# Where the first two tail loads and the last batch's turns stand in SyncE's queue

## The chip, the cores and the metric

The kernel runs on one core of a Trainium2 chip. The metric is the device time of one execution in microseconds (us). Durations inside an execution come from one profiled execution; its times count from the first instruction of the program. The engines are TensorE (PE; its weight loads are PEld), VectorE (DVE), ScalarE (ACT), GpSimd (POOL) and SyncE (SP). Each takes its instructions in the order in which the program lists them, and all of this kernel's transfers but one small one at the start are issued by SP.

## The reference

Eight batches of eight heads, 576 positions, head size 64. Retention (attention with a decaying causal mask, no softmax), then a feed-forward layer with a Swish whose slope is given for each hidden unit.

```python
scores = scale * np.matmul(q, k.transpose(0, 1, 3, 2))
gamma = 1.0 - 2.0 ** (-5.0 - np.arange(H, dtype=np.float32))
rel = pos[:, None] - pos[None, :]
Dmat = np.where(rel >= 0, gamma[:, None, None] ** rel[None, :, :], 0.0)
ret = scores * Dmat[None, :, :, :]
attn_out = np.matmul(ret, v).astype(np.float32)
x = attn_out.transpose(0, 2, 1, 3).reshape(B * S, H * D)      # 4608 x 512
h = x @ w_in                                                  # 512 -> 2048
g = h * (1.0 / (1.0 + np.exp(-beta * h)))
out = (g @ w_out).astype(np.float32)                          # 2048 -> 512
```

## The kernel before

**Blocks.** The 576 positions of a batch are cut into 512 and a rest of 64. The rests of the eight batches make a ninth block of 8 x 64 = 512 positions, the tail, so that the feed-forward layer works on nine blocks of 512 positions. They are done in the order 0 to 6, then 8 (the tail), then 7 (the last batch).

**Retention of a batch.** Queries and keys are multiplied by powers of the decay beforehand, so that a score needs only a triangular mask. The scores are worked out in chunks of 64 positions; what earlier chunks give comes through a running state (`d_st`). `scores(u)` (line 979) puts on TensorE the states' second half and the scores of batch u, and on VectorE their masks; `outputs(u)` (line 986) puts on it the products with the values, the products of the queries with the states, and the next batch's first states. For the tail (u = 8) a chunk of 128 rows holds the rests of two batches, each with its own final state.

**How inputs get there.** For each batch:

- `load_q` (line 75): two transfers of 512 KB, the queries; `pre_q` (line 282) scales them into bf16 `qs` on GpSimd.
- `load_kv` (line 87): for each of four chunks of 128 positions two transfers of 256 KB, keys and values; `pre` (line 301) casts the keys into `kn` and scales the values into `vn` on GpSimd.
- `x_q` and `x_k` (lines 338 and 343): a *turn*, a transposing DMA within the core (line 336) that makes from two chunks of `qs` the half of `qT`, from two chunks of `kn` the pair's `kT`. The scores need the turned tensors; the states need `kn` and `vn` alone.

For the tail:

- `load_tail(t)` (line 111), t = 0 to 3: six transfers of 128 KB (line 122), two each of queries, keys and values, into buffers of the ring `kvn` that the batches' chunks use too (six buffers).
- `pre` for a tail chunk (lines 310 to 320): seven GpSimd operations that scale the queries and cast the keys into one tile, and scale the values.
- `x_tail` (line 347): one turn for queries and keys together.

**The order.** Nothing is scheduled at run time: `merged` (line 796) walks through a list `fill` of feed-forward pieces and puts in other steps by a number that each carries: a step numbered x is written out ahead of the first piece whose place n is x or more. A step's instructions go to the end of each engine's queue at that point, and SP's queue is kept in exactly this order, waits included:

```python
while todo and todo[0][0] <= n:
    todo.pop(0)[1]()
f()
```

The pieces of block m are 16 `up` (first matrix and Swish, line 732) and 16 `down` (second matrix, line 766: four quarters for each of four results of 128 rows). With the last quarter of a result VectorE copies it out of PSUM (line 783) and SP stores it (line 789). Block 5 takes the places 176 to 207: its `up` pieces 176 to 191, its `down` pieces 192 to 207, and its four stores stand with the pieces 195, 199, 203 and 207. Block 6 begins at 208, the tail at 240, block 7 at 272.

**The numbers around the change.** `pair_prep` (line 1003) gives the steps of a pair of chunks their numbers, relative to `at`, the time at which the pair is due. For the last batch (b = 7) `at` is 211 for its first pair and 218 for its second; the tail's steps are set against `lo6` = 211. `scores(7)` stands at 218, `outputs(7)` at 223.5, the tail's scores at 231.5 and its outputs at 236.5. GpSimd's preparations of the last batch's four chunks stand at 191, 192, 194 and 195, those of the tail's four at 199, 203, 208 and 212.

Of the kernel before, what the change touches and what calls it, by code (L numbers as in the profile page):

```python
# [19 lines left out]
def kernel(  # L20
# [11 lines left out]
    B, H, S, D = q.shape  # L32
# [36 lines left out]
    XB = 2  # L69
# [736 lines left out]
    def F(f, *a):  # L806
        return lambda: f(*a)
# [195 lines left out]
    def pair_prep(i, at):  # L1003
        b, c = seq[i]
        if b is None:
            early, late = ((-23, -12, -7), (-18.5, -8, -6.5)) if c == 0 else ((-11, -3, 7.5), (-6, 1, 8))
            return [(lo6 + x, f) for j, at3 in enumerate((early, late))
                    for x, f in zip(at3, (F(load_tail, c + j), F(pre, i + j), F(x_tail, i + j)))]
        n, st = full.index(i), []
        if b == XB:  # L1010
            if c == 0:
                return [(d0 + 13, F(pre, i + x, (0,))) for x in range(2)] + \
                       [(d0 + 14, F(pre, i + x, (1,))) for x in range(2)]
            return [(u1 + 13.1, F(pre, i + x)) for x in range(2)]
        if c == 0:
            if b == XB + 1:
                st += [(at - 30.1, F(x_k, XB, 1)), (at - 30, F(load_kv, n)), (at - 30, F(load_kv, n + 1))]
            sooner = 4 if b == B - 1 else 0
            st += [(at - 30 - sooner, F(load_q, b, (u,))) for u in range(2)] + [(at - 20 - sooner + x, F(pre_q, b, x)) for x in range(4)]
            st += [(at - (18 if b > B - 3 else 14) + 1.5 * x, F(x_q, b, x)) for x in range(2)]  # L1020
        early = b == XB + 1 and c > 0
        loads = [] if b == XB + 1 and c == 0 else [(at - 29.7 + x / 10, F(load_kv, n + x)) for x in range(2)] if early else \
            [(at - 28 + 2 * x - (7 if b == B - 1 and c else 5 if b == B - 1 else 4 if b == B - 2 and c else 0), F(load_kv, n + x)) for x in range(2)]
        soon, turn_k = (24 if c else 20, 19 if c else 15.5) if b == B - 1 else (22, 11.5) if b == XB + 1 and c == 0 else (16, 13 if c else 11.5)
        return st + loads + [(at - soon, F(pre, i)), (at + 1 - soon, F(pre, i + 1)), (at - turn_k, F(x_k, b, c // 2))]

    for n in range(1, B - 1):
        lo, hi = (base[n] + 17, base[n + 1] - 9.5) if n == 1 else (base[n] + 3, base[n + 1] - 14)
        at = (lo, hi)
        work = [(n + 1, hi - 1, hi + 6.5)]  # L1030
        if n == B - 2:
            at = (lo, lo + 7, lo + 14, lo + 18)
            work = [(B - 1, lo + 7, lo + 12.5), (B, lo + 20.5, lo + 25.5)]
        for x, t in enumerate(at):
            streams.append(pair_prep((n + 1) * CB + 2 * x, t))
        if n == 1:
            work = []
            on_scalar.add((1, 0))
            streams.append([(base[2] - 12, F(scores_with_states, XB, XB)), (hi + 6, F(outputs, XB))])
        for u, t, t2 in work:  # L1040
            streams.append([(t, F(scores, u)), (t2, F(outputs, u))])
# [31 lines left out]
```

## Time and profile before

| | us |
|---|---|
| Three runs | 295.15, 294.44, 294.72 |
| Their median | 294.72 |
| The profiled execution | 294.68 |
| Its span, first to last instruction | 293.0 |
| Block 5, `up` from | 171.99 |
| Block 5, `down` from | 185.80 |
| Block 6, `up` from | 202.53 |
| Scores of the last batch from | 211.53 |
| Scores of the tail from | 225.67 |
| The tail's block, `up` from | 234.66 |
| Block 7, `up` from | 262.28 |

The times of blocks and scores are those of the chain of waits in order of time, the chain that ended last, followed back from the last instruction. The mean granted TensorE clock is 1.000. In the groups of the page and in the timelines a line gives start (in the timelines), duration, engine and line, operation, what is written from what, and how many instructions are put together; `SPq` is SP's queue, where the duration is that of the issue and not of the transfer. "To landing" is from the issue's start to the arrival of the data.

### The profile page before, as it was taken

What the parts mean: (1) busy time and instruction counts of PE and PEld (TensorE: products, weight loads), DVE (VectorE), ACT (ScalarE), POOL (GpSimd) and SP (SyncE); (2) the same over time, 40 slices, a digit from 0 to 9 for tenths busy, and PEclk for the clock granted to TensorE, in tenths of its full rate; (3) what the DMA queues carried; (4) which work ended last, traced back from release to release, by engine and by line L of the source; (5) the groups of instructions that cost most, each with busy time, mean ns of one, the idle gap of its engine ahead of it and who ended that gap; (6) DMA issues with size and microseconds to landing.
All of it is one profiled execution on the core that took longest, in us unless ns stands there. A gap on an engine that the chain in (4) does not pass through costs nothing.

```text
span 293.0 us, 7966 instructions
## 1 busy us (share of the span) xinstructions
PE 287.3 (98%) x3404; PEld 147.3 (50%) x3404; DVE 103.9 (35%) x223; ACT 146.5 (50%) x263; POOL 110.0 (38%) x219
## 2 busy tenths in 40 slices
PE   8899999999999999999999999999999999999995
PEld 3544456875544554455445544554554544444443
DVE  5864566606620650065105520453063500110012
ACT  5665537883487235733473348434780168007600
POOL 3956037852751914371419506773323000000000
PEclk9999999999999999999999999999999999999999
DMA  7999999999999999949999949999998110131011
GB/s 232 306 369 384 378 266 260 218 141 194 272 195 287 253 167 246 239 68 166 242 239 196 190 122 250 197 176 203 209 165 143 74 38 0 36 72 38 0 72 72
DMA packets 121986, 53.99 MB, mean 184 GB/s; under 512 B 97744, under 2 KB 114400, under 8 KB 121952
## 3 DMA queue, kind: packets, MB, share of 16 engines
q1 hardware_dynamic: 121920, 53.49, 81.3%
q8 instruction: 26, 0.43, 0.7%
q14 instruction: 8, 0.07, 0.1%
q10 hardware_dynamic: 32, 0.01, 0.0%
HBM read 36.71 MB, written 9.44 MB: 158 GB/s over the span
## 4 chain that ended last, share of the span: by engine, by line
PE 91%; DMA 5%; SPq 2%; DVE 1%; issue 0%
PE po L776 43%; PE ph L739 38%; DMA wt<-in_moe_w_in_dram 3%; PE ph L754 2%; DMA kvn<-in_v_dram 2%; PE sc L493 2%; SPq L104 2%; PE O L547 2%; PE st L515 1%; PE O L562 1%; PE ph L917 0%; SPq L84 0%; PE T L354 0%; DVE w_in_sb L214 0%; PE sc L627 0%; PE T L611 0%
## 5 line engine op out<-in xcount | busy, mean ns | idle before, releaser
L776 PE MATMUL po<-w_out_sb,gT 128*128 128x512 bf16 (+2 forms) x593 | 128.4, 373 | 0.0
L741 ACT ACTIVATE gT<-ph,beta_sb 128x512 bf16<-128x512 f32 (+1 forms) x144 | 91.3, 643 | 48.9 <-PE ph L739 48.8
L739 PE MATMUL ph<-xT,w_in_sb 128*128 128x512 bf16 (+1 forms) x576 | 113.7, 357 | 0.7 <-DVE sum L881 0.7
L776 PEld LDWEIGHTS <-gT 128*128 128x128 bf16 x593 | 56.2, 98 | 64.1
L739 PEld LDWEIGHTS <-w_in_sb 128*128 128x128 bf16 x576 | 55.9, 98 | 56.0 <-issue 0.7
L783 DVE COPY ot<-po 128x512 f32<-128x512 f32 (+2 forms) x32 | 21.5, 672 | 72.3 <-PE po L776 72.3
L499 DVE TENSOR_TENSOR R<-sc,tri 128x512 bf16<-128x512 f32 x30 | 18.7, 683 | 70.9 <-PE sc L493 70.9
L298 POOL TENSOR_TENSOR qs<-qn,gq 128x256 bf16<-128x256 f32 (+1 forms) x36 | 26.5, 765 | 35.5 <-DMA qn<-in_q_dram 35.5
L328 POOL CAST kn<-kvn 128x128 bf16<-128x128 f32 (+1 forms) x78 | 22.7, 330 | 32.4 <-DMA kvn<-in_k_dram 32.4
L308 POOL TENSOR_TENSOR vn<-kvn,gv 128x512 bf16<-128x512 f32 x26 | 27.1, 1045 | 5.1 <-DMA kvn<-in_v_dram 4.3
L576 ACT CAST xT<-O 128x512 bf16<-128x512 f32 x14 | 7.5, 589 | 32.0 <-PE O L562 32.0
L527 ACT CAST sbd<-warm 128x256 bf16<-128x256 f32 x18 | 7.3, 405 | 21.6 <-DVE warm L523 15.2
L754 PE MATMUL ph<-xT,w_in_sb 128*128 128x512 bf16 x56 | 12.6, 379 | 0.0
L523 DVE TENSOR_TENSOR warm<-st,first 128x256 f32<-128x256 f32 x20 | 8.4, 422 | 9.7 <-PE st L515 8.4
L523 DVE TENSOR_TENSOR first<-st,warm 128x256 f32<-128x256 f32 x25 | 10.6, 425 | 2.5
L576 DVE CAST xT<-O 128x512 bf16<-128x512 f32 x14 | 9.0, 687 | 5.3 <-PE O L562 5.3
L757 ACT ACTIVATE gT<-ph,beta_sb 128x512 bf16<-128x512 f32 x14 | 8.5, 687 | 4.1 <-PE ph L754 4.1
L315 POOL TENSOR_TENSOR kn<-tln,gq 128x128 bf16<-128x128 f32 (+1 forms) x12 | 5.7, 472 | 12.9 <-PE ph L739 7.1
L212 POOL CAST w_in_sb<-wt 128x256 bf16<-128x256 f32 (+1 forms) x15 | 8.0, 547 | 5.0 <-DMA wt<-in_moe_w_in_dram 5.0
L754 PEld LDWEIGHTS <-w_in_sb 128*128 128x128 bf16 x56 | 5.4, 98 | 6.2 <-POOL w_in_sb L212 0.2
L527 ACT CAST sbd<-first 128x256 bf16<-128x256 f32 x18 | 7.3, 405 | 2.2 <-DVE first L523 0.2
L229 DVE TENSOR_SCALAR w_out_sb<-wt,rbeta_sb 128x512 bf16<-128x512 f32 x13 | 5.9, 484 | 5.1 <-DMA wt<-in_moe_w_out_dram 5.1
(136 smaller groups left out, 166.9 us busy)
## 6 DMA issues: line engine op xcount, KB each, us to landing
qn<-in_q_dram SPq DMA_DIRECT2D x16, 512.0 KB, 5.3
kvn<-in_k_dram SPq DMA_DIRECT2D x32, 256.0 KB, 5.7
kvn<-in_v_dram SPq DMA_DIRECT2D x32, 256.0 KB, 5.2
out_dram<-ot SPq DMA_DIRECT2D x31, 256.0 KB, 3.7
wt<-in_moe_w_out_dram SPq DMA_DIRECT2D x8, 512.0 KB, 9.4
wt<-in_moe_w_in_dram SPq DMA_DIRECT2D x5, 512.0 KB, 10.0
wt<-in_moe_w_in_dram SPq DMA_DIRECT2D x6, 256.0 KB, 6.1
tln<-in_q_dram SPq DMA_DIRECT2D x8, 128.0 KB, 3.8
```

The lines of the kernel that those rows point to most:

```text
L298: nc.gpsimd.tensor_tensor(batch[b]["qs"][:, cs, to], q_tiles[b][:, hs, cs].rearrange("p h i d -> p i h d"), gq[:, cs, hs].unsqueeze(3).to_ ...
L308: nc.gpsimd.tensor_tensor(live[i]["vn"], kv_tiles.pop(i)[:, 1], gains(gv, c), ALU.mult)
L328: nc.gpsimd.tensor_copy(kn[:, c % 2, to], t[:, 0, hs])
L499: nc.vector.tensor_tensor(R[x][:, j].rearrange("k c p q -> k (c p) q"), sc[j].rearrange("k c p q -> k (c p) q"), mask, ALU.mult)
L523: nc.vector.tensor_tensor(new[:], add, sums[(c - 1) % 2][:], ALU.add)
L527: e((sbq[c] if c < NC - 1 else ends[u])[:], new[:])
L576: es[n % 2](x, o)
L739: nc.tensor.matmul(ph, w_in_sb[:, ko, fo * P:(fo + 1) * P], xts[m][:, ko, :, w], start=(ko == 0), stop=(ko == KO - 1))
L741: nc.scalar.activation(gts[m][:, fo, :, w], ph, ACT.Silu, scale=beta_sb[:, fo:fo + 1])
L754: nc.tensor.matmul(phs[f][:], w_in_sb[:, ko, f * P:(f + 1) * P], xts[m][:, ko], start=(ko == 0), stop=(ko == KO - 1))
L776: nc.tensor.matmul(po[:, x:y], gT[:, fo, ms, :], w_out_sb[:, fo, n0 + x:n0 + y], start=(fo == 0), stop=(fo == FO - 1), skip_group_check=m < 2)
L783: (nc.scalar.copy if m == 0 or (m, ms) in on_scalar else nc.vector.tensor_copy)(ot, po[:, :nn])
```

## The change

Four numbers in `pair_prep` are changed. No step is added or taken away, and no step itself is changed.

```diff
         if b is None:
-            early, late = ((-23, -12, -7), (-18.5, -8, -6.5)) if c == 0 else ((-11, -3, 7.5), (-6, 1, 8))
+            early, late = ((-15.9, -12, -7), (-15.85, -8, -6.5)) if c == 0 else ((-11, -3, 7.5), (-6, 1, 8))
...
-            st += [(at - (18 if b > B - 3 else 14) + 1.5 * x, F(x_q, b, x)) for x in range(2)]
+            st += [(at - (15.8 if b == B - 1 else 18 if b > B - 3 else 14) + (0.1 if b == B - 1 else 1.5) * x, F(x_q, b, x)) for x in range(2)]
...
-        soon, turn_k = (24 if c else 20, 19 if c else 15.5) if b == B - 1 else (22, 11.5) if b == XB + 1 and c == 0 else (16, 13 if c else 11.5)
+        soon, turn_k = (24 if c else 20, 22.95 if c else 18.9) if b == B - 1 else (22, 11.5) if b == XB + 1 and c == 0 else (16, 13 if c else 11.5)
```

The numbers that result:

| Step | before | after |
|---|---|---|
| First tail chunk, `load_tail(0)` | 188 | 195.1 |
| Second tail chunk, `load_tail(1)` | 192.5 | 195.15 |
| Query turns of the last batch | 193 and 194.5 | 195.2 and 195.3 |
| First key turn of the last batch | 195.5 | 192.1 |
| Second key turn of the last batch | 199 | 195.05 |

SP's queue from the last batch's last key and value load to the third tail chunk:

- before: loads of tail chunk 0, loads of tail chunk 1, two query turns, store of block 5's first result, two key turns, store of the second result, loads of tail chunk 2;
- after: first key turn, store of block 5's first result, second key turn, loads of tail chunk 0, loads of tail chunk 1, two query turns, store of the second result, loads of tail chunk 2.

From tail chunk 2 on the queue is as before: its six loads, a store, the turns of chunks 0 and 1, the loads of chunk 3, a store, the turns of chunks 2 and 3. The order on the other engines, and the buffers that the tiles take, are not touched.

## The prediction

> **What bounds the kernel now.** I read the page's busy times and its chain of waits first, then the timelines of SyncE's queue (SP), GpSimd (POOL), VectorE (DVE) and TensorE (PE) around the moved steps, and last the single turns.
>
> ```profile
> PE 287.3 (98%) x3404; PEld 147.3 (50%) x3404; DVE 103.9 (35%) x223; ACT 146.5 (50%) x263; POOL 110.0 (38%) x219
> PE 91%; DMA 5%; SPq 2%; DVE 1%; issue 0%
> ```
>
> TensorE sets the end. Only 293.0 - 287.3 = 5.7 us of the span are not matmul time, and in the chain, told in order of time, TensorE's groups join without a break from 81.17 to 289.96 us. So there is almost nothing to win behind the start; a moved transfer can only cost, and it costs when TensorE comes to something that has not landed.
>
> The queue that the change rearranges (start, duration, line, what is issued; x2 means two in a row):
>
> ```profile
> 187.50 1.81 SPq L122 DMA_DIRECT2D tln<-in_q_dram  x2
> 189.41 2.23 SPq L122 DMA_DIRECT2D tln<-in_k_dram  x2
> ...
> 193.05 1.31 SPq L122 DMA_DIRECT2D tln<-in_q_dram  x2
> ...
> 197.56 3.22 SPq L336 DMA_TRANSPOSE qT<-qs  x2
> 200.88 0.52 SPq L789 DMA_DIRECT2D out_dram<-ot  x1
> 201.51 2.66 SPq L336 DMA_TRANSPOSE kT<-kn  x2
> 204.25 0.53 SPq L789 DMA_DIRECT2D out_dram<-ot  x1
> 204.84 1.34 SPq L122 DMA_DIRECT2D tln<-in_q_dram  x2
> ...
> 212.50 2.16 SPq L122 DMA_DIRECT2D tln<-in_q_dram  x2
> 214.71 1.31 SPq L122 DMA_DIRECT2D tln<-in_k_dram  x2
> ...
> 218.15 4.26 SPq L336 DMA_TRANSPOSE kT<-kn  x2
> ```
>
> The reader is to see that SP hardly rests: from 187.50 to 218.10 one issue follows the other within 0.7 us. A tail load is 0.63 us for its 128 KB when nothing holds it, a turn 1.28. Each later issue is late by whatever is put ahead of it.
>
> ```profile
> 191.70 0.68 DVE L783 COPY ot<-po 128x512 f32<-128x512 f32 x1
> ...
> 184.81 0.88 POOL L328 CAST kn<-kvn 128x256 bf16<-128x256 f32 x3
> ...
> 190.22 0.88 POOL L328 CAST kn<-kvn 128x256 bf16<-128x256 f32 x3
> ...
> 220.86 0.29 POOL L316 CAST kn<-tln 128x128 bf16<-128x128 f32 x1
> ...
> 211.36 0.87 PE L493 MATMUL sc<-qT,kT 64*64 64x64 bf16 x64
> ...
> 225.60 0.74 PE L493 MATMUL sc<-kT 64*64 64x64 bf16 x64
> ```
>
> The copy at 191.70 makes the first result of block 5; its store (L789) stands in SP's queue between moved steps. The casts end the last batch's key pairs at 185.69 and 191.10. The matmuls at 211.36 are the last batch's scores, which need its turned queries and keys; those at 225.60 are the tail's scores, which need all four tail turns. The last of these is the closest:
>
> ```profile
> L336 SPq DMA_TRANSPOSE kT<-kn x1: 1232/1232/1232, 221.2 to 221.2; - x1
> DMA to landing us min/median/max: 4.1/4.1/4.1
> ```
>
> Issued at 221.18 (it waited for the cast that ends at 221.15), it lands at 225.3. The tail's scores go through four chunks of 16 matmuls in 0.67 us (225.67 to 226.34 in the chain), and only the last chunk reads this turn, so TensorE needs it at about 226.0. **The slack is 0.7 us**, the smallest of all moved steps.
>
> **The change, part by part.** No instruction is added or removed: 12 tail loads, two key turns and two query turns change places on SP. GpSimd's, VectorE's, ScalarE's and TensorE's order stay as they are, and so do the buffers each load takes.
>
> *The two key turns, ahead of the loads.* The first is issued at about 187.5, where the loads began: its keys are cast since 185.69. It takes 1.28 us unhindered, and 3.47 as the turn at 180.47 did behind four loads; I need not choose, since either ends by 191.0. The second is placed just behind the store of block 5's first result (fill 195), and that store waits for the copy that ends at 191.70 + 0.68 = 192.38. **This is the new wait**: before, the store came to the head at 200.88, long ready. Now SP stands idle for between 192.4 - 191.0 = 1.4 and 192.4 - 188.8 = 3.6 us, and the second key turn, 12 loads and two query turns stand behind it. The keys themselves are far too early to matter (needed at 211.4).
>
> *SP from 192.38 on.* By start to start in the rows: the store 0.63 (200.88 to 201.51); the key turn 1.38 (201.51 to 202.89); two tail chunks of six loads, 4.11 each (193.05 to the end of the waits at 197.16); two query turns, 3.72 (197.16 to 200.88) if they are hindered behind 12 loads as now, 2.76 if they go like two key turns; the second store 0.59 (204.25 to 204.84). Sum: 0.63 + 1.38 + 8.22 + 3.72 + 0.59 = 14.54, or 13.58. The third tail chunk then starts at 206.92 or 205.96, where it starts at 204.84 now: **later by 2.1 or 1.1 us**. Whether the queue's load then is nearer to the one row or the other can't be read, because it has drained during the new wait and is then filled by the same 12 loads; I take the middle, 1.6.
>
> *The tail's first two chunks.* They are issued 7 to 9 us later. Their keys land with 3.5 to 4.7 us after issue at 201 and 205; GpSimd's 1.6 us of casts (194.87 to 196.45) end by 207, and their own turns are issued about 211 and 213 either way: covered by 4 us.
>
> *The query turns.* The second is issued at 202.4 + 1.6 = about 204 to 205 instead of 199.47. Turns here land 3.1 to 6.3 us after issue, so at 207 to 211.3, against 211.36 when TensorE asks. Nothing is paid, but at the far end the cover is gone; each tenth beyond it would be a tenth of TensorE's.
>
> *What is late next.* From the third chunk on SP keeps its order: six loads, a store, two turns, six loads, a store, two turns. The last chunk's second key load (issued at 215.39) is what GpSimd's last casts (219.57 to 221.15) wait for, and they release the last turn. So 1.6 us goes through whole: the last turn lands at 225.3 + 1.6 = 226.9, and TensorE waits 1.6 - 0.7 = **0.9 us** for it. Bounds: one issue in this stretch holds SP longer than its kind (1.48 against 0.63 at 212.50); if it goes freely, the shift shrinks by 0.85, and 1.1 - 0.85 - 0.7 is below nothing, so no cost; if another load behind the query turns is held like that, 2.1 + 0.85 - 0.7 = 2.25 us. A gain is excluded to within half a microsecond: the batch's chain shows short matmul groups stretched at 195.5 (0.40 and 0.43 against 0.29 and 0.25 a batch earlier) and at 211.5 (0.70 against 0.58), 0.4 us together, all there is to recover.
>
> *TensorE behind it.* Nothing absorbs the wait: the masks, outputs and the last two blocks follow in its order, so a late 0.9 us arrives whole at the end.
>
> The sum: the profiled execution took 294.68 us (span 293.0 and 1.7 around it), against a median of 294.72; 294.68 + 0.9 = 295.6 us.
>
> **A rule weighed against the rows.** A turn's issue took 1.28 us where a load's took 0.63. The Trainium skill (Advanced Engine Details and Errata, section "X-Bar Transpose (TRN2)") says that transposing DMAs are as fast as regular ones on this chip; by that the three turns of the sum would be issued like loads, which is the rival "turns as loads" below. The traces so far speak against it as far as the issue goes.
>
> **Rivals.**
>
> *The slack holds* (not slower). One mechanism: after the drain at 189 to 192.4 SP issues the rest unhindered (query turns 1.38 each, no 1.48 load), the last turn is 0.3 to 0.7 us later than now and still lands before 226.0. For it: 206 to 208 us shows that the transfers do thin out now and then, and the rows at 187.50 and 190.05 hold backlog (1.14 and 1.59 us issues) that the wait would clear. Against it: the two turns behind 12 loads are the very sequence that was hindered. It decides below a shift of 0.7 us; the time is that of before, 294.7.
>
> *Turns as loads* (not slower). If three turns cost 0.68 each from start to start, the sum is 0.63 + 8.22 + 0.59 + 2.04 = 11.48, the third chunk starts at 203.9, 1.0 us earlier than now, and nothing is paid: 294.7. All eight turns between 197 and 222 took 1.23 us or more; little chance.
>
> *The query turns become the wait* (slower still). If they land 6.3 us after an issue at 205.5 or later, TensorE stands at the last batch's scores too; with the shift of 2.1 us and more behind it this gives 1.5 to 2.5 us: 296.2 to 297.2. For it: the one turn that took 6.3 us came behind six loads and a store. Against it: those behind 12 loads took 3.9.
>
> *The batch's small bubbles go* (faster): the 0.4 us named above, 294.3 us; only together with something that no row shows would it be past 0.2%.
>
> **How the numbers follow.** The forecast, a wait of 0.4 to 1.5 us at the tail's scores: 0.55; the slack holds: 0.26; turns as loads: 0.02; queries late: 0.12; bubbles: 0.05. A difference of 0.2%, 0.59 us, is about what a measurement of this kernel can tell. Of the forecast's case some 0.08 lies below that; so slower 0.47 + 0.12 = 0.59, same 0.26 + 0.02 + 0.08 = 0.36 (the bubbles alone give 0.01 more and the rest of theirs faster): 0.59, 0.37 and 0.04. The range must reach down to the case without a cost and up into the late queries: 294.5 to 296.6.
>
> **What would show it.** In the changed profile: a store of L789 issued at 192.4 with SP idle for 1.4 us or more before it; the third chunk's first load at 206 to 207; the last turn issued near 222.8; and a gap on TensorE ahead of or among the matmuls of L493 at about 226, with L493 in the chain longer by 0.9 us. The step fails if SP is not idle there, if the third chunk starts before 205.5, or if the last turn lands before 226.0. If TensorE stands at 211.4, the queries were the price. If TensorE's groups up to 226.3 take less than now, the forecast's sign is wrong.

## The result and the profile after

The changed kernel takes 295.40 us (median of 21 runs, 294.75 to 297.06) against 294.90 for the kernel before (21 runs, 294.44 to 295.26). The ratio is 1.0022, with a 95% interval of 1.0012 to 1.0031: some 0.65 us slower by it, 0.50 by the medians. That is little, but the interval doesn't reach 1. The runs of the changed kernel are spread over 2.3 us, those of the kernel before over 0.8. The profiled execution took 295.33 us, with a span of 293.6 (293.0 before).

The page's busy times and the chain by engine, after:

```profile
PE 286.7 (98%) x3404; PEld 146.9 (50%) x3404; DVE 104.1 (35%) x223; ACT 146.3 (50%) x263; POOL 109.7 (37%) x219
PE 84%; DMA 8%; SPq 5%; POOL 1%; DVE 1%; issue 0%; POOLq 0%
```

TensorE's work is the same, but its share of the chain has gone from 91% to 84%, and DMA, SP's queue and GpSimd have come in for what it lost. That means that the chain now leaves TensorE somewhere in the middle. In order of time (start, duration, what) it runs there like this:

```profile
217.15 4.14 DMA tln<-in_k_dram
...
222.41 0.36 POOL kn L315
...
223.03 3.60 DMA kT<-kn
226.63 0.04 issue
226.67 0.32 PE sc L493 x16
226.99 4.42 PE po L776 x20
```

Key load of the last tail chunk, its casts, its turn, and then the last 16 of the tail's 64 score matmuls. Further back the chain follows SP's issues to 204.24 and leaves them there for TensorE; that it starts with the store is read from SP's queue below and from the experiments, not from the chain. The wait ahead of the last 16 matmuls is nearly the whole change, as TensorE's timeline shows:

```profile
211.34 0.78 PE L493 MATMUL sc<-qT,kT 64*64 64x64 bf16 x64
...
225.69 0.58 PE L493 MATMUL sc<-kT 64*64 64x64 bf16 x48
226.67 0.32 PE L493 MATMUL sc<-kT 64*64 64x64 bf16 x16 [0.40 <-DMA kT<-kn]
```

The last batch's scores at 211.34 go through as before, so the query turns are in time. The tail's scores start at 225.69 (225.60 before), stop after 48 matmuls, and go on at 226.67, when the turn has landed at 226.63. Before, the 49th matmul began at 226.00. The start is 0.09 later, so the wait costs 226.67 - 226.00 - 0.09 = 0.58 us. (The bracket gives 0.40, since it counts from the modelled end of the matmuls in the pipeline.)

SP's queue, after, shows where the turn was lost:

```profile
187.08 2.27 SPq L336 DMA_TRANSPOSE kT<-kn  x1
192.43 0.36 SPq L789 DMA_DIRECT2D out_dram<-ot  x1
192.89 1.29 SPq L336 DMA_TRANSPOSE kT<-kn  x1
194.23 1.43 SPq L122 DMA_DIRECT2D tln<-in_q_dram  x2
...
203.22 2.65 SPq L336 DMA_TRANSPOSE qT<-qs  x2
205.97 0.52 SPq L789 DMA_DIRECT2D out_dram<-ot  x1
206.54 1.33 SPq L122 DMA_DIRECT2D tln<-in_q_dram  x2
...
220.98 3.77 SPq L336 DMA_TRANSPOSE kT<-kn  x2
```

Between the end of the first key turn, 187.08 + 2.27 = 189.35, and the store at 192.43 SP issues nothing for 3.1 us; it waits for the copy of block 5's first result, which ends at 191.72 + 0.68 = 192.40. The profile's list of SP's waits (us in total, times, longest) and VectorE's timeline:

```profile
SPq L789 <- DVE ot L783: 3.0, 1, 3.0
...
191.72 0.68 DVE L783 COPY ot<-po 128x512 f32<-128x512 f32 x1
```

From there it issues without a rest, and the third tail chunk starts at 206.54 instead of 204.84.

### The profile page after: what moved, and what is told of

The parts are those of the page before. It is cut to its first block, busy times and chain, and to the rows that moved or that the text cites. A ratio compares the mean times of both kernels' runs of the same rounds, so it can differ in the third digit from the quotient of the medians.

```text
span 293.6 us, 7964 instructions
## 1 busy us (share of the span) xinstructions
PE 286.7 (98%) x3404; PEld 146.9 (50%) x3404; DVE 104.1 (35%) x223; ACT 146.3 (50%) x263; POOL 109.7 (37%) x219
## 4 chain that ended last, share of the span: by engine, by line
PE 84%; DMA 8%; SPq 5%; POOL 1%; DVE 1%; issue 0%; POOLq 0%
PE po L776 40%; PE ph L739 34%; DMA wt<-in_moe_w_in_dram 3%; DMA tln<-in_k_dram 3%; PE ph L754 2%; DMA kvn<-in_v_dram 2%; SPq L104 2%; PE O L547 1%; PE st L515 1%; SPq L122 1%; PE sc L493 1%; DMA kT<-kn 1%; PE O L562 1%; SPq L336 1%; POOL kn L316 1%; POOL kn L315 0%
## 5 line engine op out<-in xcount | busy, mean ns | idle before, releaser
L776 PE MATMUL po<-w_out_sb,gT 128*128 128x512 bf16 (+2 forms) x593 | 128.4, 373 | 0.0
L776 PEld LDWEIGHTS <-gT 128*128 128x128 bf16 x593 | 56.2, 98 | 64.1
```

Of the source, the lines that this page charges most:

```text
L776: nc.tensor.matmul(po[:, x:y], gT[:, fo, ms, :], w_out_sb[:, fo, n0 + x:n0 + y], start=(fo == 0), stop=(fo == FO - 1), skip_group_check=m < 2)
```

## The experiments

The theory: that one store holds SP's queue, everything behind it is late, and TensorE pays for the last tail turn alone. The rivals: that the order itself costs (loads behind key turns, queries behind loads, crowded transfers), or that the time is lost elsewhere on TensorE. "Changed" and "before" below say which one an edit starts from.

For each profiled execution, in us: when SP starts the third tail chunk, when the last tail turn is issued and has landed, and when the last 16 score matmuls begin. The last column is the ratio of the timed runs to those of the kernel before, with its interval.

| Kernel | third chunk | turn issued | landed | last 16 from | ratio |
|---|---|---|---|---|---|
| before | 204.84 | 221.18 | 225.30 | 226.00 | |
| changed | 206.54 | 223.03 | 226.63 | 226.67, waited | 1.0022 (1.0012 to 1.0031) |
| e1, loads ahead of the store | 205.47 | 222.05 | 225.11 | 226.00 | 1.0004 (0.9995 to 1.0013) |
| e8, store alone moved back | 205.64 | 221.98 | 225.54 | 225.93 | 0.9997 (0.9988 to 1.0006) |
| e9, store ahead in the old order | 208.24 | 226.82 | 229.86 | 229.90, waited | 1.0111 (1.0073 to 1.0150) |
| e3, queries ahead of the loads | 206.96 | 223.57 | 226.66 | 226.70, waited | 1.0033 (1.0019 to 1.0047) |
| e5, loads alone moved | 205.88 | 222.00 | 225.67 | 226.20 | 1.0006 (0.9997 to 1.0015) |
| e6, turns alone moved | 205.14 | 222.44 | 225.49 | 226.13 | 1.0000 (0.9992 to 1.0009) |
| e2, changed, scores later | 207.39 | 223.51 | 226.69 | 226.95 | 1.0010 (1.0001 to 1.0020) |
| e7, changed, scores earlier | 206.91 | 223.75 | 226.84 | 226.88, waited | 1.0041 (1.0028 to 1.0053) |
| e4, before, scores later | 204.82 | 221.02 | 225.9 | 227.5 | 0.9998 (0.9990 to 1.0006) |

(For e4 the landing is 221.02 + 4.9, and the last column its scores' start, 227.14, and three quarters of their time.)

### Is it the store?

e8 changes one thing in the changed kernel: the store of block 5's first result is put aside and issued with the second one.

```diff
-            if m < 2:
+            if m < 2 or (m, ms) == (5, 0):
                 held.append((rows[:, ms, n0:n0 + nn], ot))
             else:
+                if (m, ms) == (5, 1):
+                    release(1)
                 nc.sync.dma_start(rows[:, ms, n0:n0 + nn], ot)
```

> The changed kernel with one thing different: the store of block 5's first result is issued together with that of the second, behind loads and query turns, instead of ahead of the second key turn. Theory of the idle queue (that one store holds the queue): SP waits for the cast near 190.7 at most, the last turn lands before 226.0, no wait of TensorE, ratio to before 0.999 to 1.001. Rival (the store only happens to stand there; the order of loads and turns costs): 1.0015 to 1.003.

Its SP queue:

```profile
187.62 4.61 SPq L336 DMA_TRANSPOSE kT<-kn  x2
192.28 1.43 SPq L122 DMA_DIRECT2D tln<-in_q_dram  x2
...
205.64 1.35 SPq L122 DMA_DIRECT2D tln<-in_q_dram  x2
```

Both key turns are done by 192.23 and the loads begin 2 us sooner than in the changed kernel (194.23). The ratio is 0.9997 with every other step of the change in place. So the order of loads and turns costs no time by itself; the store that stands among them did. But the order isn't without effect: in e8 SP still stands idle from 189.60 to 191.00, until the keys of the second turn are cast, and the third tail chunk starts at 205.64, 0.8 us later than before, where the changed kernel has 1.7. The last turn lands 0.39 us ahead of need instead of 0.70. The order uses up part of the slack, and the wait for the store uses up the rest.

e1 gets there by numbers alone, with the loads and the second key turn put ahead of the store:

```diff
-            early, late = ((-15.9, -12, -7), (-15.85, -8, -6.5)) if c == 0 else ...
+            early, late = ((-16, -12, -7), (-16, -8, -6.5)) if c == 0 else ...
-        soon, turn_k = (24 if c else 20, 22.95 if c else 18.9) ...
+        soon, turn_k = (24 if c else 20, 23 if c else 18.9) ...
```

> The changed kernel with the second key turn and the twelve loads put ahead of the store of block 5's first result, the query turns behind it. Theory of the idle queue (SP stands idle until the copy at 192.4 lets that store go, all behind it is late, TensorE waits for the last tail turn): SP now waits only for the cast that ends near 190.7, the third tail chunk starts at about 204.7 instead of 206.5, the last turn lands before 226.0, no wait of TensorE: ratio to the kernel before 0.999 to 1.001. Rival of the order (loads behind the key turns and queries behind the loads cost by themselves, by crowded transfers): the order is kept, so 1.0015 to 1.003 as in the changed kernel.

A ratio of 1.0004, and no wait in the profile. The third chunk starts later than expected (205.47, not 204.7), for loads were held on the way; the turn still lands 0.9 us ahead of need.

### The same store in the old order

e9 starts from the kernel before and keeps its order of loads and turns; the loads and query turns only go behind the store.

```diff
-            early, late = ((-23, -12, -7), (-18.5, -8, -6.5)) if c == 0 else ...
+            early, late = ((-15.9, -12, -7), (-15.85, -8, -6.5)) if c == 0 else ...
-            st += [(at - (18 if b > B - 3 else 14) + 1.5 * x, F(x_q, b, x)) ...
+            st += [(at - (15.8 if b == B - 1 else ...) + (0.1 if b == B - 1 else 1.5) * x, F(x_q, b, x)) ...
```

> The kernel before with the order of its loads and turns kept (12 loads, two query turns, two key turns), only the store of block 5's first result put ahead of all of them. Theory: SP idles from 187.5 to 192.4, all four turns come behind it (one more than in the changed kernel), the third tail chunk starts at 207.4 to 208.2, the last turn lands near 227.5 to 228.5, TensorE waits 1.4 to 2.5 us: ratio to before 1.005 to 1.008, more than the changed kernel's. Rival (the key turns ahead of the loads cost): 0.999 to 1.001, as the old order is kept.

The sign and the place are as the theory has them, but the ratio, 1.0111, is above what was expected. TensorE's timeline at the tail's scores:

```profile
225.87 0.45 PE L493 MATMUL sc<-kT 64*64 64x64 bf16 x32
227.41 0.32 PE L493 MATMUL sc<-kT 64*64 64x64 bf16 x16 [1.10 <-DMA kT<-kn]
229.90 0.43 PE L493 MATMUL sc<-kT 64*64 64x64 bf16 x16 [2.17 <-DMA kT<-kn]
230.67 5.30 PE L776 MATMUL po<-w_out_sb,gT 128*128 128x512 bf16 x19 [0.34 <-issue]
```

Now both of the last two turns are late. Counted by starts, as above, the last 16 matmuls would begin at 225.87 + 0.40 = 226.27 and begin at 229.90: 3.6 of the 5.2 us by which its span, 298.2, is over that of the kernel before (293.0). Another 0.3 us is there ahead of the scores (225.87 against 225.60). Most of the rest goes with another column; in stretches of 2 us: stretch, busy time of PE, PEld, DVE, ACT and POOL, then the granted clock, the DMA share and GB/s:

```profile
228.00:230.00 2.00, 0.10 (x8) 0.10 (x12) 0.00 (x0) 0.00 (x0) 0.00 (x0) 0.84 1.06 272
230.00:232.00 2.00, 1.67 (x20) 0.84 (x22) 1.29 (x2) 0.00 (x0) 0.00 (x0) 0.50 0.31 121
232.00:234.00 2.00, 2.00 (x9) 0.84 (x8) 0.00 (x0) 0.00 (x0) 0.00 (x0) 0.81 0.00 0
```

After the waits the granted clock is down to a half: 0.16 x 2 + 0.50 x 2 + 0.19 x 2 = 1.7 us of clock are missing, 0.7 of them by 230.67, while TensorE did no more than those 16 matmuls, which leaves 1.0. The feed-forward matmuls that follow (L776, up to the tail's outputs) take 5.30 us (230.67 to 235.97), where the same ones took 4.42 in the chain of the kernel before (226.34 to 230.76): 0.9 us more. The last 0.4 us lie between the scores and these matmuls. So in this profile the wait is paid for a second time. It is the profile of the longest of the six runs (299.89 us; the shortest 296.17). The mean clock of every run is on record: 0.993 or 0.994 for the three above 299 us, 0.999 or 1.000 for the three below 298. That fits a second payment in the three long runs, but where in the other two the clock fell isn't shown: e2's profile has a mean of 0.994 too, from a stretch between 5 and 15 us, long before these turns.

### Do queries behind the loads cost?

e3 puts the query turns of the changed kernel ahead of the loads, still behind the store.

```diff
-            st += [(at - (15.8 if b == B - 1 else ...) + (0.1 if b == B - 1 else 1.5) * x, F(x_q, b, x)) ...
+            st += [(at - (15.94 if b == B - 1 else ...) + (0.01 if b == B - 1 else 1.5) * x, F(x_q, b, x)) ...
```

> The changed kernel with the query turns ahead of the twelve loads, right behind the second key turn; the store and the idle time ahead of it stay. Theory of the idle queue: the same issues follow the same idle time, the third tail chunk starts at 206.3 to 206.8 and the ratio stays at 1.0015 to 1.003. Rival (the queries stand behind the loads, and that costs): ratio 0.999 to 1.001.

The ratio, 1.0033, is a little above the expected 1.0015 to 1.003, and not lower than that of the changed kernel; the intervals overlap, and whether it is worse can't be told. The third chunk starts at 206.96, a little beyond the expected 206.3 to 206.8, and the last turn is waited for again. The queries' place is not the cause.

### One half of the change at a time

The change replaces six numbers, not four: two for the loads, two for the query turns, two for the key turns. e5 takes from it only the loads, e6 only the turns.

```diff
 # e5, from before
-            early, late = ((-23, -12, -7), (-18.5, -8, -6.5)) if c == 0 else ...
+            early, late = ((-15.9, -12, -7), (-15.85, -8, -6.5)) if c == 0 else ...
 # e6, from changed
-            early, late = ((-15.9, -12, -7), (-15.85, -8, -6.5)) if c == 0 else ...
+            early, late = ((-23, -12, -7), (-18.5, -8, -6.5)) if c == 0 else ...
```

> The kernel before with only the twelve loads moved, behind the query turns and the store of block 5's first result; the two key turns stay behind them. Theory of the idle queue: SP idles until 192.4 too, but then has one turn less ahead of the third tail chunk (1.34 us), which starts at about 205.2 (204.8 before, 206.5 changed); the last turn lands 0.4 us later than before, inside the slack of 0.7: ratio 0.9995 to 1.001. Rival (late loads cost by themselves): 1.002 as in the changed kernel.

> The changed kernel with the twelve loads back at their old numbers, so that they stand ahead of the store; key turns and query turns as changed. Theory of the idle queue: SP has the loads to issue until about 198 while the copy of block 5's first result is made, so it never idles, the third tail chunk starts at about 204.8, ratio 0.999 to 1.001. Rival (earlier key turns or later query turns cost by themselves): above 1.0015.

e5's queue idles less and has one turn less to catch up with:

```profile
187.92 4.09 SPq L336 DMA_TRANSPOSE qT<-qs  x2
192.67 0.36 SPq L789 DMA_DIRECT2D out_dram<-ot  x1
193.07 1.44 SPq L122 DMA_DIRECT2D tln<-in_q_dram  x2
...
205.88 1.34 SPq L122 DMA_DIRECT2D tln<-in_q_dram  x2
```

Neither half costs anything that can be told (1.0006 and 1.0000). e5's last turn lands 0.5 us ahead of need, after a shift of the third chunk by 1.0 where 0.4 was expected: within the slack, but not by much. In e6 the loads cover the time that the store needs, and the third chunk is 0.3 us late. The cost of the change is not a sum of its parts: it takes the loads out from ahead of the store and puts three turns and the loads behind it.

### Is the last turn all that TensorE pays for?

e2 and e7 leave SP's queue of the changed kernel alone and move the tail's scores on TensorE by one feed-forward piece, 0.86 us; e4 makes e2's edit in the kernel before.

```diff
-            work = [(B - 1, lo + 7, lo + 12.5), (B, lo + 20.5, lo + 25.5)]
+            work = [(B - 1, lo + 7, lo + 12.5), (B, lo + 21.5, lo + 25.5)]      # e2 and e4
+            work = [(B - 1, lo + 7, lo + 12.5), (B, lo + 19.5, lo + 25.5)]      # e7
```

> The changed kernel with the tail's scores put one feed-forward piece (0.86 us) later on TensorE; SP's queue as in the changed kernel. Theory of the idle queue: the last turn is as late as in the changed kernel (lands near 226.6), but is asked for only at 226.9, so the wait of 0.57 us goes to 0 to 0.2: ratio to before 0.999 to 1.001. Rival (the cost lies elsewhere than at the last turn, for instance in slower matmuls or transfers): 1.0015 to 1.003.

> The changed kernel with the tail's scores one piece (0.86 us) earlier on TensorE. Theory: the last turn lands as late as in the changed kernel, TensorE comes to it 0.86 us sooner and waits 0.57 + 0.86 = 1.4 us: ratio to before about 1.005 (1.004 to 1.006). Rival (the cost isn't the wait for the last turn): unchanged, 1.0015 to 1.003.

> The kernel before with the tail's scores one piece later on TensorE. Theory: in the kernel before the last turn lands 0.7 us ahead of need, so nothing is gained: 0.999 to 1.0005. If the shift itself gained time, whatever the last turn does, this would come out below 0.998, and the run of the changed kernel with this shift would say nothing on the turn.

The scores in e2, and then in e7:

```profile
226.54 0.74 PE L493 MATMUL sc<-kT 64*64 64x64 bf16 x64
```

```profile
225.22 0.45 PE L493 MATMUL sc<-kT 64*64 64x64 bf16 x32
225.82 0.32 PE L493 MATMUL sc<-kT 64*64 64x64 bf16 x16 [0.15 <-DMA kT<-kn]
226.88 0.32 PE L493 MATMUL sc<-kT 64*64 64x64 bf16 x16 [0.74 <-DMA kT<-kn]
```

In e2 the turn lands as late as in the changed kernel (226.69), and the scores go through in one piece. In e7 it lands at 226.84, and the wait has grown and taken in the turn before it. By starts it is 226.88 - (225.22 + 0.40) = 1.26 us, against 1.4 expected and 0.58 in the changed kernel; the scores came only 0.47 us earlier in this profile (225.22 against 225.69), not 0.86. The ratios go the same way: 1.0010, 1.0022, 1.0041 as the scores go from later to earlier. Neighbouring intervals overlap; only e2's and e7's lie apart. The shift by itself gives nothing (e4, 0.9998). e2's ratio is at the upper end of what was expected, and its interval doesn't quite hold 1. In its profile the slack is only 226.95 - 226.69 = 0.26 us, so that some of its runs will have waited; that is argued, not shown.

## Why the prediction was right

The forecast was 295.6 us by a wait of 0.9 us at the tail's scores; measured are 295.40 us, and 0.58 us of wait in the profile. The store, the idle queue and the late last turn came as forecast; that the sum came so close is in part luck. Point by point:

- **TensorE sets the end, and there is nothing to win.** None of the ten other kernels is faster than the one before by more than its interval.
- **The new wait.** The store was issued at 192.43 against 192.38 forecast, and SP stood idle for 3.1 us, within the 1.4 to 3.6 given. e8 shows that this store is the cause.
- **The sum of issues behind it.** From 192.43 to 206.54 it is 14.11 us; the forecast had 13.58 to 14.54, and the middle, 1.6 us later, is close to the measured 1.70. Here luck helped: inside the sum two terms are off and nearly cancel. The two query turns took 2.75 us (203.22 to 205.97), which is the unhindered end, 0.5 below the middle of 2.76 and 3.72. The loads took 4.5 us for each chunk instead of 4.11 (194.23 to 198.74 to 203.22), 0.8 more for the two; the forecast's 4.11 was the row of the second chunk, and the first had taken 5.55 (187.50 to 193.05).
- **The queries.** In time with no wait at 211.34, as forecast: they landed 3.2 to 3.4 us after their issue, by 207.9, with 3.4 us of cover left. In e3 they stand ahead of the loads, and the cost stays.
- **The shift "goes through whole".** Here the size was off. The last turn is issued 223.03 - 221.18 = 1.85 us later, but lands only 1.33 us later: it took 3.60 us where it took 4.1 before. In between, issues were held at other places than before: the first tail turn 2.35 us instead of 1.33, the third chunk's successor 0.61 instead of 1.48 at its first load. The forecast gave both as bounds (the held load goes freely; another issue is held) and reckoned with neither; both came, the second with a turn, and nearly cancel.
- **The slack of 0.7 us** was right: with the turn at 225.67 (e5) nothing waits, at 226.63 it does. So 1.33 - 0.7 = 0.6 us, which is the wait measured.

The rival "the slack holds" is what e1, e5, e6 and e8 show, where SP stands idle for less. It holds in some runs of the changed kernel too: the shortest, 294.75 us, has a span of 293.0 us, that of the kernel before, and 8 of its 21 runs are no longer than the longest of the kernel before (295.26). "Turns as loads" fell: the eight turns of the changed profile between 187 and 225 took 1.27 to 2.35 us each to issue against 0.6 for a free load. The Trainium skill's sentence that transposing DMAs are as fast as regular ones (Advanced Engine Details and Errata, "X-Bar Transpose (TRN2)") doesn't hold for what they take of the issuing queue here.

What stays open is the spread of the changed kernel's runs. Where the turn lands so near to need, a few tenths of difference in when transfers land can go straight into the time; but the longest run, 297.06, would need a wait of over 2 us. Its mean clock is on record as 1.000, so a lower clock isn't the reason. No profile of such a run was taken.

## What to carry to other kernels

A queue that issues in order, as SP's does here, makes every store in it a gate: before moving transfers behind one, look up when its data are made, and see that the queue has enough to issue until then. Where issues follow each other without a rest, idle time of the queue is made up for only in part (here 3.1 us of it left 1.7 at the third chunk and 1.3 at the landing of the last turn), so find the transfer whose landing has the least slack, however far behind the edit it stands, and set the shift against that slack. A shift within the slack costs nothing (e5), so the same move can be free in one order and not in another.

## What the runs showed of the hardware

In e9 TensorE's granted clock fell to 0.50 for 3.4 us, from 229.3 on (worked out from the three stretches above: 0.16 x 2 / 0.50 = 0.64 us at the end of the first, the whole of the second, 0.19 x 2 / 0.50 = 0.76 us of the third), though no wait was longer than 2.2 us: in the 3.4 us before that it had worked for some 0.7, in two bursts. e7, with gaps of 0.15 and 0.74 us in the same place, kept 1.00. The Trainium skill (TensorE: Matmul & The Clock Gate, "Part 1: The HAM clock gate (the "warmup" mystery)") has the clock halved after an idle window of about 3.4 us; the length of the stretch at 0.50 agrees with such a window, and this one profile adds that the window before it need not be wholly idle.

A free 128 KB load took SP 0.63 us to issue in all profiles, but each shows single issues held for 1 us and more, at other places in each kernel. They are the likely reason why the shifts of the third chunk missed what was expected by up to 0.8 us (e1: 205.47 against 204.7).
